# Threshold attention and an ELU feed-forward on one core: idle transposes, heads in separate tiles, and a new order in the early stages

## The chip, the cores and the metric

The kernel runs on 1 core of one Trainium2 chip. The metric is the device time of one execution in microseconds (us).

## The reference

Attention in which every score further than tau below its row's maximum is dropped, then a feed-forward (FFN) block with an ELU between its two products. Everything is float32, and tau is 0.02.

```python
# q, k, v: (8 batches, 8 heads, 576, 64)
scores = np.matmul(q, k.transpose(0, 1, 3, 2)) / np.sqrt(64)
thresh = np.max(scores, axis=-1, keepdims=True) - tau
scores = np.where(scores >= thresh, scores, -1000000000.0)
attn = np.exp(scores - np.max(scores, axis=-1, keepdims=True))
attn = attn / (np.sum(attn, axis=-1, keepdims=True) + 1e-09)
x = np.matmul(attn, v)                    # -> (4608, 512)
h = x @ w_in                              # w_in (512, 2048)
g = np.where(h > 0, h, np.exp(np.minimum(h, 0)) - 1)
return g @ w_out                          # w_out (2048, 512)
```

## The kernel before

Attention goes in 32 pairs of heads, five steps to a pair: four blocks of 128 queries for both heads (i = 0 to 3, "pair steps"), and a single step i = 4 for the last 64 queries of both. In each step PE makes the scores, DVE their maxima, ACT the exponentials, DVE the masked exponentials and their sums, POOL the normalization, PE the transposes ("the turn"), ACT their copies to SBUF, and PE the product with v ("values") in two of five steps. Steps are numbered n = 5 x pair + i. Stage A is n = 0 to 19 (attention, with the first weight conversions beside it), stage B is n = 20 to 34 (attention, halves of FFN units, and the conversion of the float64 weights to float32), and behind them come the longer stages, which the change does not touch.

PE idles while DVE works, and its granted clock falls in such places (0.83 in the first pair, read below). So the kernel runs **idle transposes** of an identity matrix into the bank that the next turn will use:

```python
def room():
    rt = psum["t"].tile([P, NC, P], FP32, name="rt", tag="rt")
    for _ in range(spare.pop() if spare else 0):
        transpose(rt[:, 0], ident)
    return rt
```

In stage B both heads of a step lie in one PSUM tile, and one maximum covers both:

```python
# in scores(pr, i, hs); `apart` is empty until behind stage B
    st = open_steps[pr, i]
    if "f" in psum and not apart:
        both = psum["s"].tile([P, 2, 2, 512], FP32, name="sc")
        scs = {h: both[:, h] for h in hs}
    else:
        scs = {h: psum["s"].tile([P, 2, 512], FP32, name="sc") for h in hs}
    for a in range(2):
        for h in hs:
            k0 = a * HALF + (0 if h else TAIL)
            r, qs = (slice(h * D, (h + 1) * D), qT[:, i * P : (i + 1) * P]) if i < NC else (slice(0, P), qd)
            nc.tensor.matmul(scs[h][:, a, :HALF], qs[r], kT[r, k0 : k0 + HALF], start=True, stop=True)
    if len(hs) == 2 and "f" in psum and not apart:
        st["both"] = both
...
def exponentials(pr, i, hs):
    st = open_steps[pr, i]
    cs = slice(hs[0], hs[-1] + 1)
    src = st["both"] if len(hs) == 2 else st[hs[0]].unsqueeze(1)
    nc.vector.tensor_reduce(st["mx"][:, cs], src[:, :, :, :HALF], axis=AX.XY, op=ALU.max)
    nc.gpsimd.tensor_scalar(st["nb"][:, cs], st["mx"][:, cs], nkeep, 1.0, ALU.mult, ALU.mult)
    nc.gpsimd.tensor_scalar(st["th"][:, cs], st["mx"][:, cs], 1.0, ntau, ALU.mult, ALU.add)
    for h in hs:
        e = att.tile([P, 2, HALF], FP32, name="e")
        nc.scalar.activation(e, st[h][:, :, :HALF], AF.Exp, bias=st["nb"][:, h : h + 1], scale=keep)
        st[h] = st[h], e

def masks(pr, i, hs):
    st = open_steps[pr, i]
    cs = slice(hs[0], hs[-1] + 1)
    if hs[0] == 0:
        st["w"] = wpool[0].tile([P, 2 * S], FP32, name="w")
    w, sm, rs = st["w"], st["sm"], st["rs"]
    for h in hs:
        sc, e = st.pop(h)
        wv = w[:, h * S : (h + 1) * S].rearrange("p (a n) -> p a n", a=2)
        nc.vector.scalar_tensor_tensor(wv, sc[:, :, :HALF], st["th"][:, h : h + 1], e, ALU.is_ge, ALU.mult,
                                       accum_out=sm[:, h : h + 1])
    nc.vector.tensor_scalar(sm[:, cs], sm[:, cs], 1e-9, None, ALU.add)
    nc.vector.reciprocal(rs[:, cs], sm[:, cs])
```

Stage A has a tile for each head, and one instruction of each kind for each head:

```python
def max_of(pr, i, h):
    st = open_steps[pr, i]
    nc.vector.tensor_reduce(st["mx"][:, h : h + 1], st[h][:, :, :HALF], axis=AX.XY, op=ALU.max)

def bound_of(pr, i, h):
    st = open_steps[pr, i]
    nc.gpsimd.tensor_scalar(st["th"][:, h : h + 1], st["mx"][:, h : h + 1], 1.0, ntau, ALU.mult, ALU.add)

def exp_of(pr, i, h, on_pool=False):
    st = open_steps[pr, i]
    if not on_pool:
        nc.scalar.mul(st["nb"][:, h : h + 1], st["mx"][:, h : h + 1], nkeep)
    e = att.tile([P, 2, HALF], FP32, name="e")
    nc.scalar.activation(e, st[h][:, :, :HALF], AF.Exp, bias=st["nb"][:, h : h + 1], scale=keep)
    st[h] = st[h], e
...
# stage A, one step (loads and the conversion's other pieces cut)
for n in range(per_seq):
    pr, i = steps[n]
    hs = heads_of(i)
    x = progress[1]
    if n:
        normalize(*steps[n - 1], [0])
        turned = turn_parts(*steps[n - 1])
    max_of(pr, i, 0)
    exp_of(pr, i, 0)
    bound_of(pr, i, 0)
    if n and i not in (2, NB - 1):
        spare.append(6)
        copies = turned[0]()
    if len(hs) == 2:
        max_of(pr, i, 1)
        st = open_steps[pr, i]
        nc.gpsimd.tensor_scalar(st["nb"][:, 1:], st["mx"][:, 1:], nkeep, 1.0, ALU.mult, ALU.mult)
    if n and len(heads_of(steps[n - 1][1])) == 2:
        normalize(*steps[n - 1], [1])
    if len(hs) == 2:
        exp_of(pr, i, 1, True)
        bound_of(pr, i, 1)
    if out_values:
        out_values()
    if n and i not in (2, NB - 1):
        copies()

    if i == NB - 1 and n + 1 < per_seq:
        convert_top(x)
        convert_add(x)
        convert_abs(x)
        convert_rest(x + 1)
    elif i == 0 and n:
        convert_end(x)
        load_w()
    elif i == 1 and pr:
        convert_sign(x)
        convert_add(x)
    elif i in (2, 3):
        (prep_q if i == 2 else prep_k)(pr + 1)
        (copy_q if i == 2 else copy_k)(pr + 1)
    mask_of(pr, i, 0)

    first_scores = bool(n) and i in (2, NB - 1)
    if n and not first_scores:
        spare.append(8)
        turned[1]()()
    if n + 1 < per_seq:
        scores(*steps[n + 1], heads_of(steps[n + 1][1]))
    if n:
        for part in turned[0 if first_scores else 2 :]:
            part()()
    if len(hs) == 2:
        mask_of(pr, i, 1)
    reciprocal_of(pr, i, hs)
    out_values = None
    if n > 1 and steps[n - 2][1] in (1, NB - 1):
        out_values = values(steps[n - 2][0], 0 if steps[n - 2][1] == 1 else 1)
```

Stage B takes its FFN work in halves of 1.8 us, so many at each of three places; `parts` are the pieces of the turn of the step before, `now` the two weight pieces to convert in this step, and `valued` is true in the steps i = 1 and i = 3 (the odd steps), which also make the values that the step two before completed:

```python
first.close()
for name, bufs in (("s", 1), ("f", 2)):
    psum[name] = banks.enter_context(tc.tile_pool(name=f"ps_{name}", bufs=bufs, space=PSUM))
...
def ffn_halves(n):
    after = []
    while n and (pending or units):
        if not pending:
            if needs(*units[0]) > progress[1]:
                break
            f, a = units.popleft()
            parts, posts = f(*a)
            pending.extend((p, ()) for p in parts[:-1])
            pending.append((parts[-1], posts))
        p, posts = pending.popleft()
        p()
        after.append(posts)
        n -= 1
    return after

def finish_units(after, engines):
    for posts in after:
        for post in posts[engines]:
            post()
...
# stage B, one step
SHARES = ((2, 1, 1), (1, 1, 0), (2, 1, 0), (1, 1, 0), (2, 1, 0))
...
scores(*step, hs)
valued = steps[n - 2][1] in (1, NB - 1)
if valued:
    out_values = values(steps[n - 2][0], 0 if steps[n - 2][1] == 1 else 1)
parts = turn_parts(*steps[n - 1])
for x in now[:1]:
    convert_top(x)
finish_units(carried, slice(0, 2))
for x in now[:1]:
    convert_add(x)
copies = parts[0]()
if not valued:
    copies()
exponentials(*step, hs)
finish_units(carried, slice(2, None))
if valued:
    out_values()
    copies()
for x in now[:1]:
    convert_abs(x)
share = SHARES[n % NB]
after = ffn_halves(share[0])
finish_units(after, ACT)
for x in now[1:]:
    convert_top(x)
    convert_add(x)
    convert_abs(x)
parts[1]()()
second = ffn_halves(share[1])
finish_units(second, ACT)
if len(parts) > 2:
    parts[2]()()
carried = ffn_halves(share[2])
masks(*step, hs)
finish_units(after + second, slice(1, 2))
for x in now:
    convert_end(x)
finish_units(after + second, slice(2, None))
normalize(*step, hs)
```

## Time and profile before

| | before |
|---|---|
| time, median of 3 runs | 1376.89 us (1376.81 to 1378.41) |
| profiled span | 1373.7 us |
| stage A (to the last score product of step 20) | 106.75 us |
| stage B (to that of step 35) | 132.65 us |
| steps 35 to 44 | 74.44 us |
| steps 45 to 159 | 824.74 us |
| rest | 235.15 us |

A stage's length is read from PE's records, from the start of one step's last score product (L236) to that of a later one (stage A's from the start of the span). A step's length is taken likewise, unless maxima are named. The engines' shares of the chain that ended last, before:

```profile
PE 83%; DVE 7%; POOL 4%; ACT 3%; issue 2%; DMA 1%; SPq 0%; ACTq 0%; DVEq 0%; POOLq 0%
```

PE is busy for 1335.3 us (6748 instructions), so only its waits and its clock are left to win. PE is 83% of the chain and DVE, POOL and ACT together 14%. The first pair of heads is one of the places (columns: stretch, length, then busy us and count of PE, PE's loads, DVE, ACT and POOL, then granted clock, DMA share and GB/s):

```profile
6.60:27.00 20.40, 14.68 (x79) 11.10 (x78) 14.55 (x37) 10.07 (x19) 8.81 (x24) 0.83 0.58 125
```

Here PE waits 28% of the time and has a granted clock of 0.83.

### The profile page before, as it was taken

Reading aid. Unit: us, or ns where it says so; the run is one execution under the profiler, and the core shown is the slowest. Engines: PE = TensorE matmul, PEld = TensorE weight load, DVE = VectorE, ACT = ScalarE, POOL = GpSimd, SP = SyncE. Lnnn points to the kernel's source line nnn. Section 1 sums busy time; section 2 is a strip of 40 time slices with the busy share of each in tenths; the row PEclk is TensorE's granted clock in tenths of the full one; section 3 lists DMA queues with packets and bytes.
Section 4 is the critical chain, followed back from the end, with each engine's and each line's share of the span. In section 5 each row is a group of like instructions: output and inputs, shape, how many; then the busy total and the mean of one; then the engine's idle time right before and its main releaser. Section 6 shows DMA issues by size and latency. Waiting matters only on the chain.

```text
span 1373.7 us, 22245 instructions
## 1 busy us (share of the span) xinstructions
PE 1335.3 (97%) x6748; PEld 1003.5 (73%) x6748; DVE 1061.3 (77%) x2332; ACT 630.3 (46%) x1391; POOL 829.7 (60%) x1325
## 2 busy tenths in 40 slices
PE   7997989999999999999999999999999999999998
PEld 6664745746777777777777777777777777888886
DVE  5887885988878987888798878888888875545433
ACT  4775655325454544545453636363535442312320
POOL 4666774878647574757475647675575646525423
PEclk9999999999999999999999999999999999999999
DMA  5244452589898889798988888888889785411211
GB/s 115 59 96 138 141 148 44 183 237 260 235 256 230 250 223 267 223 260 234 250 229 246 242 245 243 217 258 220 238 234 275 220 246 167 125 67 66 92 58 31
DMA packets 316342, 259.83 MB, mean 189 GB/s; under 512 B 208320, under 2 KB 272320, under 8 KB 316224
## 3 DMA queue, kind: packets, MB, share of 16 engines
q1 hardware_dynamic: 313856, 258.13, 67.5%
q8 instruction: 54, 0.88, 0.3%
q10 hardware_dynamic: 2368, 0.30, 0.2%
q14 instruction: 64, 0.52, 0.1%
HBM read 167.84 MB, written 90.51 MB: 188 GB/s over the span
## 4 chain that ended last, share of the span: by engine, by line
PE 83%; DVE 7%; POOL 4%; ACT 3%; issue 2%; DMA 1%; SPq 0%; ACTq 0%; DVEq 0%; POOLq 0%
PE f L1091 27%; PE f L936 26%; PE sc L236 12%; PE pv L420 9%; PE rt L306 3%; PE pv L416 2%; PE f L467 2%; PE f L507 2%; DVE w L263 1%; ACT e L251 1%; DVE wtop L142 1%; POOL w L272 1%; POOL wtop L148 1%; DVE wtop L137 1%; DVE mx L276 1%
## 5 line engine op out<-in xcount | busy, mean ns | idle before, releaser
L272 POOL TENSOR_SCALAR w<-w,rs 128x576 f32<-128x576 f32 x288 | 247.6, 864 | 125.8 <-DVE rs L303 95.1
L276 DVE TENSOR_REDUCE mx<-sc 128x1 f32<-128x576 f32 x243 | 173.6, 751 | 85.7 <-PE sc L236 85.7
L296 DVE SCALAR_TENSOR_TENSOR w<-sc,th,e 128x576 f32<-128x576 f32 x243 | 191.6, 811 | 20.8 <-ACT e L287 6.5
L287 ACT ACTIVATE e<-sc,nb,keep 128x576 f32<-128x576 f32 x243 | 200.6, 831 | 8.3 <-POOL nb L610 0.7
L380 DVE STREAM_TRANSPOSE x<-w 128x512 f32<-128x512 f32 (+1 forms) x350 | 182.6, 568 | 8.2 <-POOL w L272 8.2
L285 ACT ACTIVATE nb<-mx,nkeep 128x1 f32<-128x1 f32 x227 | 67.3, 297 | 247.0 <-DVE mx L276 247.0
L236 PE MATMUL sc<-kT,qT 64*128 64x288 f32 x1024 | 164.0, 432 | 15.0 <-DVE w L263 9.1
L236 PEld LDWEIGHTS sc<-kT,qT 64*128 64x128 f32 x1024 | 91.0, 187 | 76.5 <-issue 51.8
L280 POOL TENSOR_SCALAR th<-mx,ntau 128x1 f32<-128x1 f32 x243 | 64.5, 266 | 112.0 <-DVE mx L276 111.2
L936 PE MATMUL f<-xt,sw 128*128 128x256 f32 x512 | 128.8, 389 | 0.5 <-DVE g L958 0.5
L936 PE MATMUL f<-xt,w_in_sb 128*128 128x256 f32 x512 | 124.6, 382 | 0.4 <-ACT w L950 0.2
L936 PEld LDWEIGHTS f<-xt,sw 128*128 128x128 f32 x512 | 93.3, 190 | 28.9 <-issue 13.5
L936 PEld LDWEIGHTS f<-xt,w_in_sb 128*128 128x128 f32 x512 | 96.0, 190 | 19.3 <-ACT xs L432 4.6
L1091 PE MATMUL f<-w_out_sb,s 128*128 128x256 f32 x448 | 109.4, 387 | 0.0
L1091 PE MATMUL f<-w_out_sb,g 128*128 128x256 f32 x448 | 107.6, 382 | 0.5 <-DVE g L991 0.5
L1091 PE MATMUL f<-t,s 128*128 128x256 f32 x448 | 106.6, 380 | 0.3 <-POOL s L1028 0.3
L936 PE MATMUL f<-x,w_in_sb 128*128 128x256 f32 x448 | 105.8, 379 | 0.0
L1091 PEld LDWEIGHTS f<-w_out_sb,s 128*128 128x128 f32 x448 | 82.3, 190 | 23.0 <-issue 11.3
L1091 PEld LDWEIGHTS f<-w_out_sb,g 128*128 128x128 f32 x448 | 83.8, 190 | 16.9 <-issue 3.8
L955 POOL TENSOR_TENSOR u<-u,w 128x256 f32<-128x256 f32 x64 | 49.0, 765 | 76.5 <-ACT u L950 76.5
L1091 PEld LDWEIGHTS f<-t,s 128*128 128x128 f32 x448 | 84.1, 190 | 13.7 <-POOL s L1028 2.7
L936 PEld LDWEIGHTS f<-x,w_in_sb 128*128 128x128 f32 x448 | 85.1, 190 | 11.6
(165 smaller groups left out, 2499.6 us busy)
## 6 DMA issues: line engine op xcount, KB each, us to landing
there<-x SPq DMA_DIRECT2D x500, 144.0 KB, 4.3
wTb<-there SPq DMA_DIRECT2D x75, 576.0 KB, 4.9
wTa<-there SPq DMA_DIRECT2D x50, 576.0 KB, 4.4
sw<-win_sums SPq DMA_DIRECT2D x62, 384.0 KB, 4.7
t<-wout_sums SPq DMA_DIRECT2D x45, 512.0 KB, 5.4
qm<-in_q_dram SPq DMA_DIRECT2D x128, 72.0 KB, 4.5
vm<-in_v_dram SPq DMA_DIRECT2D x64, 128.0 KB, 4.2
wst<-in_moe_w_in_dram SPq DMA_DIRECT2D x16, 512.0 KB, 4.4
```

Of the source, the lines that this page charges most:

```text
L236: nc.tensor.matmul(scs[h][:, a, :HALF], qs[r], kT[r, k0 : k0 + HALF], start=True, stop=True)
L272: nc.gpsimd.tensor_scalar(wv, wv, st["rs"][:, h : h + 1], 1.0, ALU.mult, ALU.mult)
L276: nc.vector.tensor_reduce(st["mx"][:, h : h + 1], st[h][:, :, :HALF], axis=AX.XY, op=ALU.max)
L280: nc.gpsimd.tensor_scalar(st["th"][:, h : h + 1], st["mx"][:, h : h + 1], 1.0, ntau, ALU.mult, ALU.add)
L285: nc.scalar.mul(st["nb"][:, h : h + 1], st["mx"][:, h : h + 1], nkeep)
L287: nc.scalar.activation(e, st[h][:, :, :HALF], AF.Exp, bias=st["nb"][:, h : h + 1], scale=keep)
L296: nc.vector.scalar_tensor_tensor(wv, sc[:, :, :HALF], st["th"][:, h : h + 1], e, ALU.is_ge, ALU.mult, accum_out=st["sm"][:, h : h + 1])
L380: nc.vector.transpose(x[:, :, c0 : c0 + nc_], src.rearrange("p (c g n) -> p g c n", c=nc_, n=T))
L420: nc.tensor.matmul(pv[h * D : (h + 1) * D, g0 * T : g1 * T], vm[:, h, c], wT[:, g0:g1, h * (NC + 1) + c], start=False, stop=(c == NC - 1), ...
L936: nc.tensor.matmul(loc["banks"][place], left[:, j], right[:, j], start=(begins and j == 0), stop=(j == 1), skip_group_check=True)
L955: nc.gpsimd.tensor_tensor(loc[name], x(), loc[other], op)
L1091: nc.tensor.matmul(place(m), lhs, rhs, start=(begins and v == 0), stop=(v == RU - 1), skip_group_check=True)
```

## The change

The intent: more idle transposes in the first pair, to keep the clock up there; in stage B a tile for each head, so that the first head's mask need not wait for both exponentials; one of the FFN halves right behind the scores, to fill PE's wait for the normalization; the first conversion behind the maxima in some steps; and the normalization ahead of part of the other work. The split of the PSUM costs no space: one tile of 2 x 2 x 512 values for each partition becomes two of 2 x 512 (`bufs` 2 for 1).

```diff
--- before.py
+++ after.py
@@ -601,8 +601,10 @@
             max_of(pr, i, 0)
             exp_of(pr, i, 0)
             bound_of(pr, i, 0)
-            if n and i not in (2, NB - 1):
-                spare.append(6)
+
+            first_scores = n > 2 and i in (2, NB - 1)
+            if n and not first_scores:
+                spare.append(6 if pr else 9)
                 copies = turned[0]()
             if len(hs) == 2:
                 max_of(pr, i, 1)
@@ -615,7 +617,7 @@
                 bound_of(pr, i, 1)
             if out_values:
                 out_values()
-            if n and i not in (2, NB - 1):
+            if n and not first_scores:
                 copies()
 
             if i == NB - 1 and n + 1 < per_seq:
@@ -633,11 +635,11 @@
                 (prep_q if i == 2 else prep_k)(pr + 1)
                 (copy_q if i == 2 else copy_k)(pr + 1)
             mask_of(pr, i, 0)
-
-            first_scores = bool(n) and i in (2, NB - 1)
             if n and not first_scores:
-                spare.append(8)
+                spare.append(8 if pr else 11)
                 turned[1]()()
+            elif not n:
+                idle(16)
             if n + 1 < per_seq:
                 scores(*steps[n + 1], heads_of(steps[n + 1][1]))
             if n:
@@ -668,7 +670,8 @@
         for h in heads_of(steps[per_seq - 1][1]):
             normalize(*steps[per_seq - 1], [h])
     first.close()
-    for name, bufs in (("s", 1), ("f", 2)):
+    apart.append(True)
+    for name, bufs in (("s", 2), ("f", 2)):
         psum[name] = banks.enter_context(tc.tile_pool(name=f"ps_{name}", bufs=bufs, space=PSUM))
 
 
@@ -676,7 +679,7 @@
 
     SWITCH = (NPAIR + 3) * NB
 
-    SHARES = ((2, 1, 1), (1, 1, 0), (2, 1, 0), (1, 1, 0), (2, 1, 0))
+    SHARES = ((1, 1, 1, 1), (0, 1, 1, 0), (1, 1, 1, 0), (0, 1, 1, 0), (1, 1, 1, 0))
     ACT, OTHER, ALL = slice(0, 1), slice(1, None), slice(0, None)
     with tc.manual_schedule():
         carried = []
@@ -696,40 +699,57 @@
             if valued:
                 out_values = values(steps[n - 2][0], 0 if steps[n - 2][1] == 1 else 1)
             parts = turn_parts(*steps[n - 1])
-            for x in now[:1]:
-                convert_top(x)
+
+            behind_max = valued or n == per_seq
+            if not behind_max:
+                for x in now[:1]:
+                    convert_top(x)
             finish_units(carried, slice(0, 2))
-            for x in now[:1]:
-                convert_add(x)
+            if not behind_max:
+                for x in now[:1]:
+                    convert_add(x)
+            share = SHARES[n % NB]
+            early_ = ffn_halves(share[0])
             copies = parts[0]()
             if not valued:
                 copies()
-            exponentials(*step, hs)
+            for h in hs:
+                max_of(pr, i, h)
+                exp_of(pr, i, h)
+                bound_of(pr, i, h)
             finish_units(carried, slice(2, None))
+            if behind_max:
+                for x in now[:1]:
+                    convert_top(x)
+                    convert_add(x)
             if valued:
                 out_values()
                 copies()
             for x in now[:1]:
                 convert_abs(x)
-            share = SHARES[n % NB]
-            after = ffn_halves(share[0])
+            finish_units(early_, ACT)
+            after = ffn_halves(share[1])
             finish_units(after, ACT)
+            after = early_ + after
             for x in now[1:]:
                 convert_top(x)
                 convert_add(x)
                 convert_abs(x)
             parts[1]()()
-            second = ffn_halves(share[1])
+            second = ffn_halves(share[2])
             finish_units(second, ACT)
             if len(parts) > 2:
                 parts[2]()()
-            carried = ffn_halves(share[2])
-            masks(*step, hs)
-            finish_units(after + second, slice(1, 2))
+            carried = ffn_halves(share[3])
+            for h in hs:
+                mask_of(pr, i, h)
+            reciprocal_of(pr, i, hs)
+            finish_units(after, slice(1, 2))
+            normalize(*step, hs)
+            finish_units(second, slice(1, 2))
             for x in now:
                 convert_end(x)
             finish_units(after + second, slice(2, None))
-            normalize(*step, hs)
             if i in (2, 3):
                 (prep_q if i == 2 else prep_k)(pr + 1)
                 (copy_q if i == 2 else copy_k)(pr + 1)
@@ -749,7 +769,6 @@
     assert progress[1] == len(pieces)
     assert units[0][1][0] == 1 and not pending
     banks.close()
-    apart.append(True)
     for name, bufs, stack in (("f", 3, ctx), ("s", 2, banks), ("t", 1, banks)):
         psum[name] = stack.enter_context(tc.tile_pool(name=f"ps_{name}2", bufs=bufs, space=PSUM))
     early.close()
```

## The prediction

> **What bounds the kernel now.** The page first: PE is busy for 97% of 1373.7 us and carries 83% of the chain that ended last. So time is to be had only where PE waits or runs slowly. The stretches view finds these places. Its columns are length, then busy time and count of PE, PE's loads, DVE, ACT and POOL, then the granted clock, DMA share and GB/s.
>
> ```profile
> 0.00:8.00 8.00, 5.73 (x28) 5.49 (x28) 1.47 (x3) 1.28 (x1) 1.27 (x10) 1.00 0.79 111
> 8.00:32.00 24.00, 19.09 (x111) 14.34 (x111) 17.05 (x43) 13.07 (x24) 11.05 (x27) 0.86 0.58 128
> ...
> 105.50:142.00 36.50, 27.71 (x150) 18.54 (x150) 29.89 (x55) 22.32 (x46) 25.40 (x28) 0.95 0.49 134
> 142.00:186.00 44.00, 39.98 (x209) 28.03 (x209) 37.67 (x72) 27.33 (x55) 31.71 (x37) 1.00 0.49 138
> 186.00:226.00 40.00, 36.97 (x158) 18.59 (x157) 33.54 (x61) 23.07 (x45) 27.22 (x31) 0.96 0.30 88
> ...
> 313.00:1138.00 825.00, 822.91 (x4197) 621.35 (x4196) 703.79 (x1607) 404.10 (x916) 527.80 (x881) 1.00 0.86 242
> ```
>
> After 313 us PE is idle for 2 of 825 us. The change touches only what lies before 240 us: stage A (attention steps n = 0 to 19, about 0 to 107 us) and stage B (steps 20 to 34, with FFN halves between, 107 to 239.8 us). The other 1134 us should stay as they are.
>
> I cut stage B at the starts of the DVE maxima, 107.19, 115.74, ... 219.88 us for steps 20 to 33. Over these 13 steps, 112.7 us, DVE is busy 97.2 us and PE 96.8 us: 86% each. **Neither is full; they wait for each other.** The timeline of DVE in one step shows how:
>
> ```profile
> 150.95 1.35 DVE L246 TENSOR_REDUCE mx<-sc 128x2 f32<-128x1152 f32 x1
> 152.22 0.62 DVE L137 TENSOR_SCALAR wtop<-wst 128x512 uint32<-128x512 uint32 x1
> 152.87 0.69 DVE L142 SCALAR_TENSOR_TENSOR wtop<-wst,wtop 128x512 uint32<-128x512 uint32 x1
> 154.66 0.82 DVE L263 SCALAR_TENSOR_TENSOR w<-sc,th,e 128x576 f32<-128x576 f32 x1 [1.10 <-ACT e L251]
> ```
>
> DVE idles 1.10 us before the first mask. The waits view over those 13 steps (engine, line and who it waited for: total us, times, longest):
>
> ```profile
> ACT e L251 <- POOL nb L247: 34.2, 13, 4.4
> DVE w L263 <- ACT e L251: 12.5, 13, 1.1
> POOL w L272 <- DVE rs L266: 12.3, 10, 1.8
> PE sc L236 <- DVE w L263: 8.2, 6, 4.5
> ```
>
> The 12.5 us are 13 equal waits: the first mask starts 1.66 us after the first exponential, that is after both exponentials (1.55 us), because both heads lie in one tile. In stage A, with a tile for each head, it starts 0.95 us after the first (10.41 to 11.36).
>
> PE's own gaps between 107 and 239 us sum to 15.8 us in its timeline:
>
> ```profile
> 112.42 2.29 PE L236 MATMUL sc<-kT,qT 64*128 64x288 f32 x8 [4.46 <-DVE w L263]
> ...
> 150.03 0.66 PE L306 MATMUL rt<-ident,w 128*128 128x128 f32 x4 [1.14 <-POOL w L272]
> ...
> 183.20 0.63 PE L306 MATMUL rt<-ident,w 128*128 128x128 f32 x4 [1.73 <-ACT xt L427]
> ...
> 200.33 1.58 PE L236 MATMUL sc<-kT,qT 64*128 64x288 f32 x8 [1.91 <-DVE w L263]
> ```
>
> [...] half rate shows in stretches of 3.4 us (13.4 to 16.8, 23.6 to 27.0, 112.4 to 115.7, 201.1 to 204.4 us)[...]. [...] before 8.0 us PE ran nothing but 28 transposes, yet 6.6 to 13.3 us was granted 1.00. [...] the normalization (L272) takes 0.74 us in quiet stretches of stage A and 1.12 us on average in stage B. [...] the bound on ACT (L285) takes 297 ns for one element[...].
>
> **The change part by part.**
>
> *Stage A, first pair.* 16 idle transposes in step 0; 9 and 11 for 6 and 8 in steps 1 to 3; step 2 takes the ordinary order (turn first, scores after). Added: 16 + 2x6 + 20 = 48 transposes. Eight take 1.04 us at full clock and 1.56 us at half, so about 0.11 us each: 5.3 us of PE work, mostly in idle time. What it buys is the clock:
>
> ```profile
> 9.29:13.24 3.95, 1.36 (x10) 0.70 (x6) 3.23 (x9) 1.85 (x3) 0.78 (x3) 1.00 0.84 140
> 13.24:18.91 5.67, 5.67 (x33) 4.75 (x31) 3.30 (x10) 3.02 (x5) 2.98 (x6) 0.70 0.75 223
> 18.91:22.83 3.92, 1.91 (x9) 1.01 (x9) 3.85 (x9) 2.11 (x4) 1.90 (x6) 1.00 0.16 27
> 22.83:29.64 6.81, 6.51 (x38) 5.50 (x38) 3.99 (x11) 4.70 (x9) 3.04 (x7) 0.75 0.65 123
> ```
>
> These are steps 0 to 3. Steps 1 and 3 are PE-bound at a clock of 0.70 and 0.75; the third pair's step 2 takes 4.71 us at 1.00. At full clock I lay step 1 out as 9 idle + 4 + 11 idle + 4 transposes and the scores: 4.7 us (-1.0). Step 2, now with 20 idle transposes: 4.5 us (+0.6). Step 3, its turn no longer held back by late copies: 4.4 us (-2.4). Sum -2.8 us; I count **-2.3**, as a half-rate window may remain.
>
> *Conversion behind the maxima.* Step 20's first conversion now runs on DVE and POOL as early as 92.6 us, inside step 17, which takes 5.99 us (90.56 to 96.55) against 4.71 for the same step of the third pair. Behind a maximum that needs stage B's scores it cannot run so early. I expect **-0.8** of the 1.28 us there; the ACT piece hoisted at 91.7 us stays. The work returns in step 20 (0.42 + 0.69 us on DVE), where it fills the wait for the exponentials, so step 20 gains little.
>
> *Heads apart.* Removed in each pair step: one maximum of 1.35 us, the bound on POOL (0.27 to 0.44 us, behind a 1.29 us POOL addition in the steps with an early conversion). Added: two maxima at a pitch of 0.70 us (1.42 together, +0.07), two bounds of 0.30 us on ACT (5.2 us busy of 8.8 a step), a second threshold on POOL. From the first maximum, exponential 1 ends at 0.76 + 0.1 + 0.3 + 0.83 = 2.0 us, while DVE is busy with maxima and a conversion until 1.42 + 1.31 = 2.7 us. So the 1.10 us wait goes: 11 pair steps x 1.1 = 12 us of DVE idle time.
>
> That is not 12 us of time, since PE must keep up. In each step I take the larger of DVE and PE busy: 7.3, 7.4, 8.9, 8.3, 7.5 | 8.9, 9.4, 8.8, 7.6, 6.8 | 7.5, 8.7, 6.4, together 103.5 us. Adding 0.8 us for split maxima and 1.1 us for the returned conversion makes 105.4 against 112.7: **-7.3**.
>
> *The early half unit of FFN.* The shares sum to the same (4, 2, 3, 2, 3 halves); counting them against the weights converted gives 33 halves in both orders, so no work moves across the border. The half of 1.81 us fills the wait of 0.8 to 1.1 us for POOL's normalization in the even steps. This lets PE reach the busy time that the sum above assumes; it is not added again. The normalization also comes before the conversion's end.
>
> *Half-rate windows of stage B.* At 112 us the scores take 2.29 us for 1.24, at 201 us the scores and values lose about 1.6 us. The second may vanish with its 1.91 us gap, the first hardly: **-0.8**.
>
> Against this I set **+0.7** for new collisions[...] in the odd steps, where two conversions on POOL now come back to back. Sum: -2.3 - 0.8 - 7.3 - 0.8 + 0.7 = -10.5. From 1376.9 this is 1366.4 us.
>
> **The rivals.** (1) *PE's order takes the wait over.* Its queue is in order, and the second score matmul needs head 2's mask; the early half needs a bank whose ELU comes after the conversion's end, about 2.2 us after the last mask by DVE's rows (0.4 + 1.2 + 0.6). For it: DVE and PE are equally loaded, so a small slip shows. Against it: in most steps PE, not the mask, is late. Stage B would then gain 3 us and the whole 1371 us. (2) *POOL or ACT becomes the bound* through more small instructions[...]. POOL is busy 5.8 us of 8.8 on average, up to 7.4: room, but not beside conversion; 1373 us. (3) *Stage A's idle transposes lie on the path:* the chain of waits runs through 20 to 22 of them in later pairs (49.43 us, 2.62 us). If the clock does not hold, 48 more cost up to 3 us: 1371 us. (4) *Everything fits* and both cold windows vanish: -15 us, 1362 us.
>
> **Range and chances.** Were every PE gap (15.8 us), the cold loss of stage B (3) and stage A's 3.6 us won, it would be 1354 us, only 1.6% faster. So over 2% is almost excluded. Slower by 2% would take 27 us, more than a second wait in every step. Range 1360 to 1372.5 us: faster 0.01, within 2% 0.98, slower 0.01.
>
> **What would show it.** Right: clock 1.00 from 6.6 to 27 us; the fifth step's maximum near 27 us for 29.64; no conversion before stage B's first maximum; first mask after its own exponential, with the 12.5 us wait under 3; stage B's length near 124 us for 132.7; an unchanged rest. Wrong: a POOL or ELU wait of about 1 us before PE's early half; masks waiting for thresholds from POOL; a longer stretch after 240 us.

## The result

| | before | after |
|---|---|---|
| time, median (range) of 4 runs | 1377.65 us (1376.81 to 1379.33) | 1368.7 us (1367.16 to 1372.33) |
| profiled span | 1373.7 us | 1366.1 us |
| stage A | 106.75 | 103.22 |
| stage B | 132.65 | 130.92 |
| steps 35 to 44 | 74.44 | 74.44 |
| steps 45 to 159 | 824.74 | 822.39 |
| rest | 235.15 | 235.15 |
| PE's gaps in stage B | 15.8 | 8.5 |
| half rate in stage B | 6.8 | 13.7 |

The ratio of the times is 0.9937 [0.9914, 0.9960], a change within 2%; outputs are correct. Ratios here are the mean time of one kernel's runs over that of the other's of the same rounds, so not quite the ratio of the medians.

The same line of the page after the change:

```profile
PE 89%; DVE 4%; ACT 2%; POOL 2%; issue 1%; DMA 0%; ACTq 0%; DVEq 0%; POOLq 0%; SPq 0%
```

PE is busy for 1340.4 us (6796 instructions; the 48 new ones are the idle transposes). The chain runs through PE more than before (89% for 83%): the waits for the other engines have become fewer. The stretches view after, first pair and then the three five-step parts of stage B:

```profile
6.60:27.00 20.40, 18.77 (x141) 15.55 (x141) 16.74 (x43) 11.61 (x22) 8.90 (x25) 1.00 0.58 127
...
103.20:144.50 41.30, 34.97 (x180) 24.26 (x178) 39.80 (x72) 30.01 (x63) 30.11 (x35) 0.92 0.53 145
144.50:190.00 45.50, 45.14 (x206) 29.16 (x207) 40.64 (x77) 30.60 (x63) 32.28 (x37) 0.96 0.52 136
190.00:234.50 44.50, 42.55 (x192) 23.21 (x190) 28.46 (x57) 26.01 (x60) 22.42 (x28) 0.96 0.27 78
```

The first pair now has its full clock. In stage B PE is fuller but slower: the trace grants either 1.00 or 0.50 there (0.50 from 107.03 to 113.86 us, 1.00 from 113.90 to 144.50), so a mean of 0.92 over 41.30 us means 2 x 0.08 x 41.30 = 6.6 us at half rate, and 3.6 us in each of the other parts. The records give four windows of 3.4 us, two together from 107.0 us, and one each from 144.6 and 195.8 us. The first pair's PE timeline (start, length, engine, line, operation and shape, count, in brackets the idle time before it and its releaser) shows how the idle transposes (`rt<-ident` without `w`) close it, here at the end of step 1:

```profile
15.03 1.36 PE L306 MATMUL rt<-ident 128*128 128x128 f32 x11
16.23 0.60 PE L306 MATMUL rt<-ident,w 128*128 128x128 f32 x4
16.77 1.24 PE L236 MATMUL sc<-kT,qT 64*128 64x288 f32 x8
```

The bracket of idle time is missing in all three lines: PE did not wait, and the eight score products take their 1.24 us of full clock. In stage B PE's timeline has these lines, the score products of steps 21 and 25 and the early FFN half of step 25:

```profile
108.59 2.99 PE L236 MATMUL sc<-kT,qT 64*128 64x288 f32 x8 [4.16 <-DVE w L296]
...
141.23 1.71 PE L236 MATMUL sc<-kT,qT 64*128 64x288 f32 x8
144.56 3.67 PE L467 MATMUL f<-xt,w_in_sb 128*128 128x256 f32 x8 [1.62 <-DVE g L481]
```

The first eight score products take 2.99 us where 1.24 is their full rate. Those of step 25 take 1.71 us at full clock: they start on head 1's tile and stand in front of head 2's, which step 24's mask leaves only at about 141.65 us. Then the early half waits 1.62 us for a bank that the ELU (`g`, L481) must leave, and a half-rate window begins with it: 3.67 us where 1.89 us is usual. The turn of the step before stands behind all this, at 148.07 us.

DVE's timeline shows what heads apart are for, in step 22, and what spoils them, in step 32:

```profile
122.84 0.69 DVE L142 SCALAR_TENSOR_TENSOR wtop<-wst,wtop 128x512 uint32<-128x512 uint32 x1
123.45 0.81 DVE L296 SCALAR_TENSOR_TENSOR w<-sc,th,e 128x576 f32<-128x576 f32 x1
...
206.38 1.42 DVE L276 TENSOR_REDUCE mx<-sc 128x1 f32<-128x576 f32 x2 [0.49 <-PE sc L236]
...
210.49 0.82 DVE L296 SCALAR_TENSOR_TENSOR w<-sc,th,e 128x576 f32<-128x576 f32 x1 [1.63 <-POOL wtop L148]
```

In step 22 the mask follows the conversion at once. In step 32 it waits 1.63 us. The view names a POOL addition, but ACT's timeline of the same moment shows the exponential that the mask also needs, done only at 210.38 us:

```profile
208.73 0.58 ACT L322 COPY wTa<-rt 128x512 f32<-128x512 f32 x1 [2.10 <-PE rt L306]
...
209.55 0.83 ACT L287 ACTIVATE e<-sc,nb,keep 128x576 f32<-128x576 f32 x1
```

ACT idled 2.10 us for the turn's transposes, with the copy of them ahead of the exponential in its queue. DVE's first maximum was there at about 207.1 us. The turn was late because the early half now stands before it on PE.

### The profile page after: what moved, and what is told of

Same layout as the page of the kernel before. It is cut to its first block, busy times and chain, and to the rows that moved or that the text cites.

```text
span 1366.1 us, 22394 instructions
## 1 busy us (share of the span) xinstructions
PE 1340.4 (98%) x6796; PEld 1008.9 (74%) x6796; DVE 1064.7 (78%) x2344; ACT 638.5 (47%) x1418; POOL 825.2 (60%) x1322
## 4 chain that ended last, share of the span: by engine, by line
PE 89%; DVE 4%; ACT 2%; POOL 2%; issue 1%; DMA 0%; ACTq 0%; DVEq 0%; POOLq 0%; SPq 0%
PE f L1110 28%; PE f L955 28%; PE sc L236 13%; PE pv L420 9%; PE f L507 3%; PE rt L306 3%; PE pv L416 3%; PE f L467 2%; DVE mx L276 1%; POOL w L272 1%; DVE w L296 1%; ACT e L287 1%; DVE wtop L142 0%; ACT wTa L322 0%; DVE wtop L137 0%
## 5 line engine op out<-in xcount | busy, mean ns | idle before, releaser
L276 DVE TENSOR_REDUCE mx<-sc 128x1 f32<-128x576 f32 x270 | 192.8, 750 | 89.0 <-PE sc L236 88.8
L296 DVE SCALAR_TENSOR_TENSOR w<-sc,th,e 128x576 f32<-128x576 f32 x270 | 212.8, 811 | 26.7 <-ACT e L287 10.0
L287 ACT ACTIVATE e<-sc,nb,keep 128x576 f32<-128x576 f32 x270 | 223.0, 831 | 9.2 <-POOL nb L612 0.7
L285 ACT ACTIVATE nb<-mx,nkeep 128x1 f32<-128x1 f32 x254 | 75.2, 296 | 256.4 <-DVE mx L276 256.4
L280 POOL TENSOR_SCALAR th<-mx,ntau 128x1 f32<-128x1 f32 x270 | 75.7, 281 | 114.0 <-DVE mx L276 113.3
L1110 PEld LDWEIGHTS f<-t,s 128*128 128x128 f32 x448 | 84.1, 190 | 13.7 <-POOL s L1047 2.7
```

What stands on the lines that cost most here:

```text
L1110: nc.tensor.matmul(place(m), lhs, rhs, start=(begins and v == 0), stop=(v == RU - 1), skip_group_check=True)
```

## The experiments

Twelve runs on three chips, each correct. All but the fifth were timed against the kernel before on the same chip, in 5 rounds (6 runs each, 5 for e12). One profile each; stage lengths come from it, and the last column is the length of steps 45 to 159, where all these kernels have the same code.

| run | time, median (range) | ratio to before | A | B | 45 to 159 |
|---|---|---|---|---|---|
| before, first profile | 1377.65 | 1 | 106.75 | 132.65 | 824.74 |
| after, first profile | 1368.7 | 0.9937 | 103.22 | 130.92 | 822.39 |
| e1 first pair only | 1372.66 (1371.83 to 1373.15) | 0.9951 [0.9933, 0.9969] | 104.17 | 132.91 | 824.16 |
| e2 no early half | 1365.33 (1364.06 to 1369.46) | 0.9904 [0.9883, 0.9925] | 103.90 | 126.47 | 827.41 |
| e3 conversion first | 1368.94 (1366.87 to 1372.51) | 0.9927 [0.9905, 0.9948] | 103.18 | 129.24 | 822.89 |
| e4 heads together | 1372.45 (1371.34 to 1375.49) | 0.9955 [0.9934, 0.9975] | 103.45 | 132.75 | 823.08 |
| e5 before again | 1379.62, one run | | 108.22 | 132.92 | 826.99 |
| e6 after again | 1368.21 (1367.17 to 1369.50) | 0.9917 [0.9894, 0.9941] | 103.35 | 130.92 | 822.74 |
| e7 early half in the fifth step only | 1365.49 (1364.56 to 1366.33) | 0.9896 [0.9873, 0.9919] | 103.40 | 128.26 | 822.53 |
| e8 copies behind | 1367.56 (1365.82 to 1369.45) | 0.9913 [0.9887, 0.9940] | 103.28 | 126.65 | 824.49 |
| e9 idle transposes in the gaps | 1368.17 (1365.86 to 1370.87) | 0.9917 [0.9890, 0.9944] | 103.39 | 126.98 | 824.99 |
| e10 all three | 1370.63 (1368.22 to 1373.65) | 0.9934 [0.9908, 0.9959] | 103.20 | 130.46 | 823.21 |
| e11 together, no early half | 1371.58 (1370.48 to 1373.54) | 0.9940 [0.9916, 0.9963] | 103.25 | 133.16 | 822.45 |
| e12 fifth and copies | 1366.48 (1366.03 to 1366.86) | 0.9902 [0.9877, 0.9927] | 103.99 | 126.61 | 823.82 |

The kernel before itself scatters more than most of the others: 1374.53 to 1382.85 us in 11 runs beside e1 to e4, 1375.80 to 1386.43 beside e5 to e8, 1376.66 to 1387.79 beside e9 to e12, with medians of 1378.65, 1379.07 and 1379.02.

### e1: the first pair alone

The kernel before with the stage A hunks of the change only (idle 16, spare 9 and 11, `first_scores`).

> The kernel before with the changes of stage A alone (16, 9 and 11 idle transposes, ordinary order in step 2). Theory: the fifth maximum comes at 26.8 us for 29.6, the shift of -2.8 us stays up to stage B, step 17 keeps its 5.99 us, stage B keeps its 132.7 us, so the whole is 2 to 3.5 us under the kernel before (ratio about 0.998). Rival (all of the -8.9 us but noise comes from stage B's order): within 1 us of the kernel before.[...]

Measured: 1372.66 us, ratio 0.9951, so 6 us less on this chip; in its trace the span fell by 2.7 us against the first profile of before, and stage A by 2.6 us. So the trace is as the theory has it, and the timed gain is larger than its 2 to 3.5 us. The clock is 1.00 from 6.6 to 27 us, with PE busy for 18.63 of 20.40 us.

Step 17 stayed at 6.0 us (87.95 to 93.95), as in before, so the shorter step 17 of the whole change does belong to the conversion behind the maxima. Its six runs lie within 1.3 us, those of before beside it within 8.3 us.

### e5 and e6: both kernels once more, as a measure of scatter

No edit in either.

> The kernel before, unchanged, for a second trace. Theory (stages A to C repeat to some tenths, only the stretch after them scatters by 2 us or so, as it was 823.2 to 828.2 us in five traces of the same code): stage A 106.5 to 107.9 us, stage B 131.5 to 134 us, the two half-rate windows of the first pair there again. Rival ([...]the first trace was a lucky or an unlucky one): stage A or B differs by 1.5 us or more.

> The changed kernel, unchanged, on this chip beside the next two. Theory: ratio 0.993 to 0.995 to the kernel before, stage A about 103.5 us, stage B 130 to 132 us with step 25 of 12 us or so (from last score to last score) each time. Rival (the 12.3 us of step 25 came from one unlucky clock window): step 25 near 10.5 us and stage B under 130 us.

After's second profile agrees with its first: stage B 130.92 us in both, windows at 107.2, 144.7 and 195.9 us for 107.0, 144.6 and 195.8. Before's second profile has a stage A of 108.22 us, 1.5 us longer than its first, with half rate from 9.4 to 19.6 us: the clock from 6.6 to 27 us is 0.75 for 0.83. All the changed kernels reach the last score product of step 5 between 29.9 and 30.5 us; before took 32.8 and 34.2 us. So the idle transposes took away not only a loss but one whose size differs from run to run. That fits e1's larger gain in time than in the first traces, though two profiles do not show the whole spread.

The waits of PE in the later, unchanged code are another part of the scatter (engine, line, who it waited for: total, times, longest). Before has this one in its first profile:

```profile
PE pv L416 <- DMA wTa<-there: 1.2, 1, 1.2
```

Its second profile has three such waits for transfers, 2.6 us together. After has no wait of PE for a DMA there in either profile. Summed over the steps that are at least 0.25 us longer than the shortest of all runs, as the excess over it, steps 45 to 159 lose 2.35 and 3.9 us in before, 0 and 0 in after, 4.7 in e2, 2.1 in e9, 2.0 in e8, 1.3 in e12, and 0 in e7 and e11.

### e2: no early half

```diff
-    SHARES = ((1, 1, 1, 1), (0, 1, 1, 0), (1, 1, 1, 0), (0, 1, 1, 0), (1, 1, 1, 0))
+    SHARES = ((0, 2, 1, 1), (0, 1, 1, 0), (0, 2, 1, 0), (0, 1, 1, 0), (0, 2, 1, 0))
```

> The changed kernel with the early half unit put back behind the first transposes (shares 0,2,1,1 / 0,1,1,0 / 0,2,1,0 / 0,1,1,0 / 0,2,1,0). Theory (the early half fills PE's wait for the normalization in the even steps, but in step 25 it waits 1.62 us for the bank and helps to bring a half-rate window): gaps of 0.8 to 1.2 us come back in steps 22, 25, 27 and 32, about +3 us, less about 2 us if the half-rate window at 144 us goes: 0 to 3 us slower than the changed kernel. Rival (the early half is a net loss): 1.5 us or more faster than the changed kernel. Rival (as predicted, it lets PE reach its busy time): 4 us slower.

Measured: 1365.33 us, ratio 0.9904, and stage B at 126.47 us, 4.45 us shorter than after's. In time it is some 3 us under after (1368.7 and 1368.21 us, on other chips), so the first rival came true, the early half as a net loss, and not the theory. The two single windows of half rate are gone; the pair at 107.4 us stays. The second part in the stretches view of e2:

```profile
143.50:188.00 44.50, 42.45 (x208) 27.28 (x208) 41.04 (x78) 31.59 (x66) 33.59 (x38) 1.00 0.53 139
```

PE has more idle time there than after (2.05 us of 44.50, after 0.36 of 45.50), a clock of 1.00 for 0.96, and comes through sooner. In step 32 ACT's timeline has the copy early, and the exponential at 205.68 us, not behind a late turn:

```profile
204.29 0.59 ACT L322 COPY wTa<-rt 128x512 f32<-128x512 f32 x1 [0.33 <-PE rt L306]
...
205.68 0.83 ACT L287 ACTIVATE e<-sc,nb,keep 128x576 f32<-128x576 f32 x1
```

The mask follows at 207.11 us without a wait, and the step takes 6.29 us for 7.31. In single steps the early half does what it was for: step 24 takes 8.10 us with it and 9.34 without, step 29 7.42 and 8.90. But DVE does not pass it on: the first maxima of steps 24 and 25 are 8.52 us apart with it and 8.54 without, and step 25 is longer by more, 12.30 us for 9.35. This run's steps 45 to 159 were the longest of all (827.41 us), so its one profile shows little of the gain; the median of six runs does.

### e4: heads together again

`apart.append(True)` back behind stage B, one tile of both heads, and the maxima, bounds, exponentials and masks of both heads as before; everything else as after.

```diff
-    apart.append(True)
-    for name, bufs in (("s", 2), ("f", 2)):
+    for name, bufs in (("s", 1), ("f", 2)):
...
-            for h in hs:
-                max_of(pr, i, h)
-                exp_of(pr, i, h)
-                bound_of(pr, i, h)
+            exponentials(*step, hs)
...
-            for h in hs:
-                mask_of(pr, i, h)
-            reciprocal_of(pr, i, hs)
+            masks(*step, hs)
```

> The changed kernel with both heads in one tile again (one maximum, bounds on POOL, both exponentials ahead of the masks), all else as changed. Theory (the heads' parting takes DVE's 1.1 us wait out of 11 pair steps, of which PE lets about half through): stage B 4 to 7 us longer than the changed kernel's 131.4 us. Rival (PE's order and clock had eaten it all): stage B within 1.5 us of the changed kernel. Prediction as it stood: 8 us longer or more.

Measured: 1372.45 us, ratio 0.9955, stage B 132.75 us. With the early half in place, heads apart are worth 132.75 - 130.92 = 1.8 us of stage B, less than the 4 to 7 us of the theory. In time it is about 4 us (1368.21 and 1368.7 us with heads apart, on other chips). After's trace has two half-rate windows more than e4's, so 1.8 us may be too few for heads apart alone.

### e11: heads together and no early half

The edits of e4 and e2 both.

> The changed kernel with both heads in one tile and with no early half (so of stage B's parts only the conversion's place and the order of the normalization are left). Theory (the parting of the heads is worth about as much as DVE's wait that PE lets through, and the early half had hidden it): stage B 131 to 133 us against 126.9 us of the same without the early half and with the heads apart. Rival (parting the heads does nothing; the order of the normalization did it): 127 to 128 us.

Measured: 1371.58 us, ratio 0.9940, stage B 133.16 us. Against e2, heads apart are worth 133.16 - 126.47 = 6.7 us. This is the two-by-two that the explanation needs:

| stage B, us | early half | no early half |
|---|---|---|
| heads together | 132.75 (e4) | 133.16 (e11) |
| heads apart | 130.92 (after) | 126.47 (e2) |

| time, us (ratio to before) | early half | no early half |
|---|---|---|
| heads together | 1372.45 (0.9955) | 1371.58 (0.9940) |
| heads apart | 1368.21 and 1368.7 (0.9917 and 0.9937) | 1365.33 (0.9904) |

The first table is of single profiles, and half-rate windows differ among them: 6.8 us in e4, 10.2 in e11, 13.7 in after, 6.8 in e2. The window that e11 has more than e2 lies in step 27, which takes 10.81 us there and 10.02 in e4 without it, so about 0.8 us of the 6.7 may be the clock. The times agree that heads apart gain, and that the early half costs where heads are apart, but not on how much the one hides of the other: by medians, across chips, heads apart are worth about 4 us with the early half and 6 without, and by ratios 2.5 to 5.2 and 5.0. PE's gaps in stage B, the bracketed idle times of its timeline summed, are the clearest: 16.7 us in e4, 15.2 in e11, 8.5 in after, 8.7 in e2. Heads apart halve them, and the early half does not lessen them.

The waits view of DVE over stage B, for e11, then e2, then after, shows where the 6.7 us come from:

```profile
DVE w L263 <- ACT e L251: 9.8, 9, 2.1
```

```profile
DVE w L296 <- ACT e L287: 2.3, 3, 1.4
```

```profile
DVE w L296 <- ACT e L287: 5.5, 6, 3.1
...
DVE w L296 <- POOL wtop L148: 1.6, 1, 1.6
```

The mask's wait falls from 9.8 to 2.3 us with heads apart alone. With the early half it comes back to 5.5 and 1.6 us, the latter the one read above as a wait for ACT. But 3.5, 2.3 and 4.0 us of these lie in the last two steps (33 and 34), which are as long in all three runs within 0.1 us, so there they cost nothing. Over the 13 steps before them the same view has, for e11 and then after (e2 has no such wait):

```profile
DVE w L263 <- ACT e L251: 6.3, 7, 1.1
```

```profile
DVE w L296 <- POOL wtop L148: 1.6, 1, 1.6
DVE w L296 <- ACT e L287: 1.5, 3, 1.1
```

Before had 12.5 us in these steps. So half of that wait was already gone with the new order of conversion and normalization, without making stage B shorter (133.16 us), and heads apart took the other half.

### e7: the early half in the fifth step only

```diff
-    SHARES = ((1, 1, 1, 1), (0, 1, 1, 0), (1, 1, 1, 0), (0, 1, 1, 0), (1, 1, 1, 0))
+    SHARES = ((0, 2, 1, 1), (0, 1, 1, 0), (0, 2, 1, 0), (0, 1, 1, 0), (1, 1, 1, 0))
```

> The changed kernel with the early half in the single-head steps alone (shares 0,2,1,1 / 0,1,1,0 / 0,2,1,0 / 0,1,1,0 / 1,1,1,0). Theory (in the pair steps the early half pushes the turn back, ACT's copies of the turn stand ahead of its exponentials, and so the masks come late; in the single step it fills a real wait of 1.4 to 1.8 us): stage B 125 to 127 us, 4 to 6 us under the changed kernel and up to 1.5 us under the variant with no early half (126.9 us). Rival (the early half is bad everywhere): slower than the variant with none. Rival (the difference was a clock window): within 1.5 us of the changed kernel.

Measured: 1365.49 us against 1368.21 us of the unchanged after on the same chip, and the two ranges do not touch. The mean of e7 over that of after, of the same rounds, is 1365.43 / 1368.35 = 0.9979. Stage B is 128.26 us, also 2.7 us less. Steps 45 to 159 were alike in both (822.53 and 822.74). So the early half in the pair steps costs 2.7 us, in trace and in time. That is less than the theory's 4 to 6 us. The trace has all of it in the last five steps: steps 20 to 29 together are as long as after's within 0.02 us, and the rest is 2.66 us shorter, of which step 32 gives 1.02 (6.29 us for 7.31) and step 31, where the window at 195.8 us is missing, 1.63 (8.89 for 10.52).

e7 also shows what the early half of the single step does. Step 25 has no early half here, and still its PE timeline reads:

```profile
144.76 0.66 PE L306 MATMUL rt<-ident,w 128*128 128x128 f32 x4 [1.64 <-POOL w L272]
145.26 5.31 PE L467 MATMUL f<-xt,w_in_sb 128*128 128x256 f32 x16
```

PE, quicker through step 24, waits 1.64 us for the normalization where after waited 1.62 us for a bank, and the half-rate window follows too (5.31 us for 3.62). The gap in step 25 comes from the single step's early half, and the pair step's half only changes what ends it. e7 is, with e2, the fastest version measured; its ratio to before is 0.9896.

### e8: the turn's copies behind the exponentials

```diff
             copies = parts[0]()
-            if not valued:
-                copies()
             for h in hs:
...
             if valued:
                 out_values()
-                copies()
+            copies()
```

> The changed kernel with ACT's copies of the turn behind the exponentials in all steps, the early halves kept. Theory (the loss of the early half in pair steps is ACT's order): the waits of the first mask in steps 25 and 32 (1.08 and 1.63 us) go, stage B 128 to 129.5 us. Rival (the bank wait of step 25 and the half-rate window that follows are the loss): step 25 stays at 12 us and stage B within 1 us of the changed kernel.

Measured: the wait in step 32 is gone and stage B is 126.65 us, but the time is 1367.56 us, only 0.65 us under e6, with ranges that overlap. In step 25 PE's timeline is at first after's, to 0.03 us (scores at 141.20 for 141.23), up to this:

```profile
144.56 1.99 PE L467 MATMUL f<-xt,w_in_sb 128*128 128x256 f32 x8 [1.62 <-DVE g L481]
```

The same gap at the same time was not followed by half rate here (1.99 us for 3.67), where it was in both profiles of after (windows from 144.6 and 144.7 us), so the kernel alone does not decide it. Nor does the length of the gap: one of 1.73 us (before, from 181.47) and one of 1.78 us (e2, from 135.50) were followed by full rate (the next FFN products take 1.88 and 3.62 us, as usual), while 1.22 us were followed by after's window at 195.8 us. The traces of before and after show where the windows start: in after at 107.03, 144.57 and 195.77 us, which is 11 and 26 times 3.413 us from the first, and in before at 13.38, 23.62, 112.37 and 201.11 us, 3, 29 and 55 times 3.413 us from the first. Why none follows e8's gap the runs do not show.

So this one trace is in favour of the theory (copies ahead of the exponentials hold up the masks) for step 32, and the time does not confirm that undoing it pays. Against e6, stage B is 4.3 us shorter in the trace, but 1.7 us of that are the half-rate window of step 25 that did not come (its last transposes are at 148.55 us for 150.23) and 1.6 us the one of step 31; step 32 gives 1.0. Steps 45 to 159 are 1.75 us longer, and the rest behind them 0.8 us (235.93 us for 235.15; e10 and e12, with the same edit, have this too, and why is not known).

### e3: the conversion first in the odd steps again

```diff
-            behind_max = valued or n == per_seq
+            behind_max = n == per_seq
```

> The changed kernel with the first conversion ahead of the maxima again in the odd steps (behind them only in step 20). Theory (behind the maxima, both conversions lie back to back and the second pass of L142 takes 1.67 us for 0.69 beside POOL's addition): L142 falls from a mean of 954 ns to near 806 ns, DVE wins about 1 us in each of five odd steps, but the maxima start about 1 us later after the scores; sum within 1.5 us of the changed kernel. Rival (the move is what the odd steps gain from): 3 us or more slower, with the 1.7 us waits of PE for ACT's copies of the values back in steps 23 and 28.

Measured: 1368.94 us, ratio 0.9927, the same as after. The groups view over 103 to 240 us (line, engine, operation, shape, count, busy us, mean ns, idle before) for after and then e3 (before has 25 with a mean of 806 ns):

```profile
L142 DVE SCALAR_TENSOR_TENSOR wtop<-wst,wtop 128x512 uint32<-128x512 uint32 x26 | 24.8, 954 | 0.9
```

```profile
L142 DVE SCALAR_TENSOR_TENSOR wtop<-wst,wtop 128x512 uint32<-128x512 uint32 x26 | 20.6, 791 | 0.9
```

The move costs DVE 4.2 us of longer instructions: two conversions then come back to back, and the second collides with the first's addition on POOL. In after's step 23 such a one takes 1.67 us for 0.69, beside a POOL addition of 1.35 us from 130.63:

```profile
130.86 1.67 DVE L142 SCALAR_TENSOR_TENSOR wtop<-wst,wtop 128x512 uint32<-128x512 uint32 x1
```

The time did not fall, for PE loses about what DVE wins: with the conversion first, steps 21, 23 and 28 take 8.62, 9.52 and 9.53 us for 7.42, 8.54 and 8.53, and PE's waits for ACT's copies of the values are back in steps 23 and 28 (1.27 and 1.29 us), which the rival had said; steps 24 and 27 are 0.75 us shorter each. That the traced stage B was 1.7 us shorter comes from steps 25 and 31 (2.0 and 1.1 us less), where e3 has no half-rate window, and the time does not repeat it.

### e9: idle transposes in stage B's gaps

After, with 36 idle transposes at the end of step 20, 14 ahead of the early half of step 25, and 10 at the end of step 30:

```diff
+            if n == per_seq + 5:
+                idle(14)
             early_ = ffn_halves(share[0])
...
             carried = ffn_halves(share[3])
+            if n in (per_seq, per_seq + 10):
+                idle(36 if n == per_seq else 10)
```

> The changed kernel with idle transposes where its trace shows PE waiting: 36 in step 20, 14 in step 25, 10 in step 30. They add no work that is waited for; they only keep PE busy. Theory (three half-rate windows cost stage B 2.9 + 1.8 + 1.6 us there): no half-rate window between 100 and 230 us, scores of step 21 in 1.3 us for 2.99, stage B 124.5 to 126.5 us, 4 to 6 us faster than the changed kernel. Rival (what the clock loses, waits on DVE make up anyway): stage B 129 us or more. Rival (the idle transposes hold PE's queue up): slower than the changed kernel.

Measured: all half-rate windows are gone, and the mean clock is 1.00 in each of its three parts, for 0.92, 0.96 and 0.96. Stage B is 126.98 us, 3.9 us shorter than after's. But the time is 1368.17 us and the ratio 0.9917, that of e6. In the trace, steps 25 and 31 are 1.67 and 1.63 us shorter than after's (10.63 for 12.30, 8.89 for 10.52) and step 20 by 0.8, while step 32 stays at 7.31. The traced run had 2.2 to 2.6 us more in steps 45 to 159 than after's two. So the windows, with what the idle transposes cost, are worth some 4 us of stage B in that trace, and the run does not show that this reaches the end: inconclusive.

### e12 and e10: the parts put together

e12 is e7 with e8. e10 is e12 with the idle transposes of e9.

> The changed kernel with the early half in single-head steps alone and ACT's copies of the turn behind the exponentials. Theory (both repair the same loss, ACT's late exponentials, so they do not add up): stage B 125 to 127 us apart from a half-rate window in step 25 (1.8 us), time within 1.5 us of the variant with the early half in the fifth step alone. Rival (they add up): 2 us or more faster than it.

> The previous variant with the idle transposes in steps 20, 25 and 30 as well: the version that the experiments point to. Theory: stage B 122 to 125 us with no half-rate window, 3 to 5 us faster than the previous variant, 1361 to 1364 us, ratio to the kernel before 0.985 to 0.989. Rival (idle transposes gain nothing once the exponentials are early): within 1 us of the previous variant.

e12 measured 1366.48 us, ratio 0.9902: no better than e7. That is as the theory has it, because both remove the same late exponentials. e10 was **a miss**: 1370.63 us, slower than e12. Its PE timeline at the end of step 20 against that of e9:

```profile
106.76 5.82 PE L306 MATMUL rt<-ident 128*128 128x128 f32 x36 [2.35 <-ACT wTb L322]
112.50 1.24 PE L236 MATMUL sc<-kT,qT 64*128 64x288 f32 x8
```

```profile
105.12 4.15 PE L306 MATMUL rt<-ident 128*128 128x128 f32 x36 [0.52 <-ACT wTb L322]
109.20 1.46 PE L236 MATMUL sc<-kT,qT 64*128 64x288 f32 x8
```

The idle transposes write into a bank of the turn, and with the copies behind the exponentials that bank comes free late. In e10 they wait 2.35 us for ACT's copy, then run into a half-rate window (from 108.1 us), take 5.82 us for e9's 4.15, and hold up the scores of step 21: step 20 takes 10.15 us, in e12 7.68. Nor did the half-rate windows go, which its theory had said: e10 has two, from 108.1 and 121.7 us. Idle transposes that should fill a gap were themselves the last thing before the scores.

## Why the prediction was right, and where it was not

The total was right: 1368.7 us lies in the range of 1360 to 1372.5, 2.3 us above the point. Its parts were not all right, and that they summed so well is partly luck. The sum by parts, all from stage lengths of the traces:

| term | predicted | measured | from |
|---|---|---|---|
| first pair | -2.3 | -2.8 | maximum of step 4 at 26.82 us for 29.64 |
| conversion out of step 17 | -0.8 | -0.8 | step 17: 5.15 us for 5.99 |
| heads apart (sum by larger of DVE and PE) | -7.3 | -6.7 | e11 to e2 |
| collisions of conversions, order | +0.7 | +0.5 | before to e11, stage B |
| early half | 0 | +4.5 | e2 to after, stage B |
| half-rate windows of stage B | -0.8 | in the three rows above | 6.8 us before, 10.2 e11, 6.8 e2, 13.7 after |
| unchanged code | 0 | -2.4 | steps 45 to 159 |
| sum | -10.5 | -7.6 | spans 1373.7 and 1366.1 |

The two rows of stage A sum to 3.6 us and its length fell by 3.5 us. The rows of stage B are differences of single profiles, so a few tenths in each mean nothing, and a half-rate window of 3.4 us more or less can be up to 1.7 us (an estimate, half its length, from the 0.50 that the trace grants in it).

**The first pair was right**, by its own lay-out rather than its discount: "Sum -2.8 us; I count -2.3" has measured 2.8. By steps, laid out 4.7, 4.5 and 4.4 us, the maxima of steps 1 to 4 at 13.34, 18.04, 22.52 and 26.82 us give 4.70, 4.48 and 4.30. The clock is 1.00 from 6.6 to 27 us. Rival (3), that the clock would not hold, is out: it was 1.00 in all twelve profiles of kernels with the new first pair. What was not foreseen is that before's own first pair differs from run to run (32.8 and 34.2 us to step 5), so that the timed gain of e1 is larger than that of the two first traces.

**Heads apart was right in size in the traces, but only without the early half**: 6.7 us for 7.3, some 0.8 us of it perhaps the clock. The reading behind it, that DVE's first mask waited for both exponentials because of the common tile, is shown by the wait falling from 6.3 us to none in the 13 steps between e11 and e2. Two readings of it were off: the "13 equal waits" are ten of 1.1 us and three of 0.38, 0.70 and 0.38, and half of the 12.5 us went with the order alone (12.5 in before, 6.3 in e11).

**The early half is the step that failed.** The prediction said of it: "This lets PE reach the busy time that the sum above assumes; it is not added again." The runs showed in its place that it fills no wait on balance: PE's gaps in stage B sum to 8.5 us with it and 8.7 without (16.7 and 15.2 with heads together), and PE then runs more of its work at half rate (13.7 us for e2's 6.8). As measured it costs 4.5 us of stage B (e2 to after): 1.8 us by the halves in the single steps (e2 to e7), which the time does not confirm (1365.33 and 1365.49 us, on two chips), and 2.7 us by those in the pair steps (e7 to after), which it does. What the traces show of it:

- Queues in order. In after's step 25 the normalization is done at 144.52 us, but the turn, behind the half on PE, starts at 148.07; in step 32 ACT idles 2.10 us with the turn's copy ahead of the exponential. The half stands before the turn on PE, the turn's copy stands before the exponentials on ACT. So a half of 1.81 us that was to fill a wait on PE of about 1 us delays the exponentials, and DVE waits: 1.63 us in step 32, 1.08 us in step 25. In step lengths this is 1.0 us, step 32. My sum took the larger of two busy times for each step, which assumes that neither engine's order makes the other wait. e8, which turns the order on ACT around, removes the wait of step 32.
- A gap that moved. In step 25 the half waits 1.62 us for the ELU of an earlier one. The prediction named this wait ("an ELU wait of about 1 us before PE's early half"), but e7 shows that it only stands in the place of one for the normalization: what PE won in the single step, it waits in the next.
- The clock. After this wait, and at 195.8 us, there is a half-rate window that e2 doesn't have. Two windows of 3.4 us at half rate cost at most 3.4 us of PE work, an estimate from the windows' lengths. The steps agree: e9, with the early halves and without windows, gains 1.67 and 1.63 us in steps 25 and 31 and nothing in step 32; e7 and e8 gain 1.0 us there. So in the traces some three quarters of the 4.5 us are the clock, and in e8 one of the two windows, that of step 25, did not follow the same gap of 1.62 us. In time only e7's 2.7 us are confirmed; e9, which wins the 3.3 us of the clock in its trace, is no faster than after.

So rival (1) took place in part: it said that stage B would gain 3 us and the whole would be 1371 us; stage B gained 1.7. The expectation "the 12.5 us wait under 3" failed by little over the same 13 steps (1.5 and 1.6 us, 3.1 together) and "stage B's length near 124 us" clearly (130.92).

**Half rate in stage B** went the other way than -0.8. The first window was to stay ("the first hardly") and has become two, with a gap of 4.16 us before the scores of step 21; the one at 201 us has its successor at 195.8 us, and one is new. Part of this is not the change: before's second profile also has two windows at step 21 (from 111.8 us) and none at 201.

**The collisions of conversions** were near in time, +0.5 in stage B, and clearer as an instruction's length (954 ns for 806). e3 shows that undoing this move wins nothing that can be measured in time.

**The unchanged rest** was right for steps 35 to 44 and the end (74.44 and 235.15 us in both), and wrong for steps 45 to 159, which lost 2.4 us in the first pair of profiles. The excess of single steps, PE's waits for transfers among it, was 2.35 us in before and 0 in after, and as much as 4.7 in e2. Code and order are the same there. Why these waits fall as they do stays open: of the changed kernels the four with the shortest stage B (e2, e8, e9, e12) have 823.8 to 827.4 us there and the others 822.4 to 823.2, but before and e1, with a long stage B, have 824.2 to 827.0. It is of the size of e8's and e9's gains in stage B, so a single trace cannot tell what those are worth.

The total thus came out right partly by luck, since errors cancelled: stage B gained 5.7 us less than predicted, stage A 0.4 more, and the unchanged code gave 2.4 that nobody had asked for. Beside e6, where before was slower by its own scatter, the ratio is 0.9917, or 11.5 us between the means.

## What to carry to other kernels

Before work is moved into an engine's wait, follow what stands behind it in the in-order queues of the engines that it feeds: a filler longer than the wait, ahead of a producer, can cost more than the wait did (here a half of 1.81 us for waits of about 1 us, and then a wait of 1.63 us on DVE), and a sum of busy times will not show it. Test the parts of a change in a two-by-two, since a good part (6.7 us of the traced stage B here) can be hidden in part by another; and look at the times as well as at single profiles, for here the times show less of it than the profiles. The granted clock of the first pair rose from 0.83 to 1.00 with 48 idle transposes and the new order of its step 2, and half-rate windows came behind gaps of 1.22 and 1.62 us as well as of 4.16: look for short gaps as well as for long ones, read the length of one known instruction to see the rate, and count half-rate windows before two profiles are compared.
